# Experts 4 to 7 of a routed expert layer: all rows in one wide pass, behind both passes of experts 0 to 3

## Chip, cores and metric

The kernel runs on one core of one Trainium2 chip. The metric is the device time of one execution in microseconds; times are compared by the median of several runs.

## The reference, cut to what matters

The first half is a chunked state-space scan (Mamba-2 style) that gives 3072 tokens of 256 features. The second half routes each token to one of eight experts and is where the change is:

```python
def _moe_ref(x, w_gate, w1, w2):          # x: (3072, 256), w1: (8, 256, 1024), w2: (8, 1024, 256)
    logits = x @ w_gate
    expert_idx = np.argmax(logits, axis=1)
    logits_shift = logits - logits.max(-1, keepdims=True)
    probs = np.exp(logits_shift)
    probs /= probs.sum(-1, keepdims=True) + 1e-09
    gate_w = probs[np.arange(N), expert_idx]
    for e in range(E):
        mask = expert_idx == e
        h = np.maximum(x[mask] @ w1[e], 0.0)
        out[mask] = gate_w[mask, None] * (h @ w2[e])
```

With the inputs of this case the experts 0 to 7 get 372, 343, 418, 417, 336, 365, 415 and 406 tokens. All matmuls of the expert part are in float32.

## The kernel before, in words

**Scan and placing.** The scan runs over 12 steps of two chunks (the loop over `d`). As tokens are finished, their expert is chosen, their place among that expert's rows is counted (`rank`, `ranked`), and GpSimd writes each row by an indirect DMA (`place`, `to_places`) into `x_hbm`, a buffer in device memory with a region of NR rows for each expert. A row carries 256 features, the logits' parts and the token's number. Behind the last row of each expert, `empty_rest(e)` writes 128 empty rows, also by an indirect DMA from GpSimd; it must wait for the earlier reads of `x_hbm`, and a later read of `x_hbm` waits for it.

**Passes.** Every expert's rows are worked in two passes: the first takes 256 rows (P1), the second up to 192 more (P2). `jobs` lists them: jobs 0 to 7 are the first passes of experts 0 to 7, jobs 8 to 15 the second passes. A job goes through these steps:

- `m_load(i)` issues on SP's queue four DMAs for the rows (`xb`), one for their gate parts and token numbers (`lt`), and, for the first of a pair of second passes, two more (`lh`) for the rows behind the last full tile.
- `m_xT(i)` transposes `xb` to `xT` on VectorE in blocks of 32 by 32. For a second pass it transposes both jobs of the pair and then computes three gates (`gates`: VectorE, an exponential on ScalarE, VectorE again).
- The up stage: `up` makes two matmul calls for each of the 8 blocks of the hidden dimension, and ScalarE writes `hT` by a relu. In the trace each float32 matmul call is two instructions, so one expert's up stage is 32 instructions.
- The down stage `m_y(i)`: eight matmul calls for each tile of 128 rows, scaled by the gate (`put`) and sent to the output by an indirect DMA from GpSimd (`send`).

For second passes, `m_pair` handles two experts and has 17 programs for 128 to 192 rows in steps of 4. `over` computes the number of the program from the counts; TensorE and ScalarE load it (`number_of`) and branch. Rows above the full tile of 128 are done for both experts together in one half tile (`m_half`); there is none where the program's size is 128.

**Order.** The order of instructions on each engine is the order of the code; each engine works its own queue in that order. In the loop over `i` that does the first passes, a function `between(f)` is called behind the relu of block `f`. At `f == FT // 2` it issues, in this order: the weights of expert `i + 2` where they aren't there yet, the empty rows of two experts (`i` from 1 to 4), `m_load(i + 3)`, the load of a program number, and `m_xT(i + 1)`. So a first pass is loaded three experts ahead and transposed one ahead. Behind the first passes come four turns of `m_pair`, the loads and transposes of later pairs, and `m_y` of both jobs.

**Buffers.** `xb` and `xT` have four buffers, `lt` seven, `hT` three, `yo` (output tiles) three; PSUM has four banks for the up stage and two for the down stage. The weights of experts 0 to 2 have tiles of their own; those of experts 3 to 7 lie in memory that the scan has given up.

Of the kernel before, what the change touches and what calls it, by code (L numbers as in the profile page):

```python
# [38 lines left out]
SIZES = list(range(128, P2 + 1, 4))  # L39
SLACK, FEW = 64, 64  # L40
NR = N + 512
EW = 3
# [5 lines left out]
def ssd_then_moe(ctx, tc, xs_in, ae_in, wgx, w_gate, w1, w2, gx, gb, gc, ga, out):  # L48
# [41 lines left out]
    size_no = route.tile([1, E // 2], I32, name="size_no")  # L90
    steps = route.tile([1, len(SIZES) - 1], FP32, name="steps")
    spare = route.tile([1, 1], FP32, name="spare")
# [68 lines left out]
    def empty_consts():  # L161
        nc.gpsimd.memset(zrows, 0.0)
        none = sm.tile([128, 1], I32, name="none")
        nc.gpsimd.iota(none, pattern=[[0, 1]], base=N, channel_multiplier=0)
        nc.gpsimd.tensor_copy(zrows[:, TOK:TOK + 1].bitcast(I32), none)
        at_i = sm.tile([128, E], I32, name="at_i")
        nc.gpsimd.iota(at_i, pattern=[[NR, E]], base=0, channel_multiplier=1)
        nc.gpsimd.tensor_copy(at_r, at_i)
        steps_i = sm.tile([1, len(SIZES) - 1], I32, name="steps_i")
        nc.gpsimd.iota(steps_i, pattern=[[SIZES[1] - SIZES[0], len(SIZES) - 1]], base=P1 + SIZES[0],  # L170
                       channel_multiplier=0)
        nc.gpsimd.tensor_copy(steps, steps_i)
# [274 lines left out]
    def over():  # L447
# [9 lines left out]
        over_ = sm2.tile(sh, FP32, name="over")  # L457
        nc.vector.tensor_tensor(out=over_, in0=bc(most[:, :, None], sh), in1=bc(steps[:, None, :], sh), op=ALU.is_gt)
        nc.vector.tensor_reduce(most, over_, axis=AX, op=ALU.add)
# [15 lines left out]

    jobs = [(0, e) for e in range(E)] + [(1, e) for e in range(E)]
    ex = [dict() for _ in jobs]

    def m_load(i, engs=(nc.sync,)):

        p, e = jobs[i]
        r0, n = e * NR + P1 * p, (P1, P2)[p]
        xb = mo.tile([128, P1 // 32 * 64], FP32, name="xb", bufs=4)
        for c in range(4):
            engs[c % len(engs)].dma_start(out=xb[32 * c:32 * c + 32, 0:2 * n].rearrange("p (r z) -> p r z", z=64),
                              in_=x_hbm[r0:r0 + n, 64 * c:64 * c + 64].rearrange("(r j) z -> j r z", j=32))
        ex[i]["xb"] = xb[:, 0:2 * n].rearrange("p (r i k) -> p k r i", k=KT, i=32)
        lt = mo.tile([128, 2, MID], FP32, name="lt", bufs=7)[:, 0:2 - p]
        nc.sync.dma_start(out=lt, in_=x_hbm[r0:r0 + 128 * (2 - p), DM:W].rearrange("(t p) w -> p t w", p=128))
        ex[i]["lt"] = lt  # L490
        if p and e % 2 == 0:
            lh = mo.tile([128, 1, MID], FP32, name="lh", bufs=3)
            for u in range(2):
                q = r0 + u * NR + 128
                nc.sync.dma_start(out=lh[64 * u:64 * u + 64, 0], in_=x_hbm[q:q + 64, DM:W])
            ex[i]["lh"] = ex[i + 1]["lh"] = lh

    def gates(mid, n):

        sh = [128, n, E]  # L500
        l = mo.tile([128, 2, E], FP32, name="t_l", bufs=2)[:, 0:n]
        logits(l, mid)
        mx = mo.tile([128, 2], FP32, name="t_mx", bufs=2)[:, 0:n]
        nc.vector.tensor_reduce(mx, l, axis=AX, op=ALU.max)
        sub = mo.tile([128, 2, E], FP32, name="t_sub", bufs=2)[:, 0:n]
        nc.vector.tensor_tensor(out=sub, in0=l, in1=bc(mx[:, :, None], sh), op=ALU.subtract)
        nc.scalar.activation(sub, sub, func=ACT.Exp)  # L507
        se = mo.tile([128, 2], FP32, name="t_se", bufs=2)[:, 0:n]
        nc.vector.tensor_reduce(se, sub, axis=AX, op=ALU.add)  # L509
        nc.vector.tensor_scalar(out=se, in0=se, scalar1=1e-9, scalar2=None, op0=ALU.add)  # L510
        gt = mo.tile([128, 2], FP32, name="t_gt", bufs=8)[:, 0:n]
        nc.vector.reciprocal(gt, se)
        return gt

    def m_xT(i):
        p, e = jobs[i]
        n = (P1, P2)[p]
        for j in range(i, i + 1 + p):
            ex[j]["xT"] = mo.tile([128, KT, P1], FP32, name="xT", bufs=4)
            nc.vector.transpose(ex[j]["xT"][:, :, 0:n].rearrange("p k (r j) -> p k r j", j=32), ex[j]["xb"])  # L520
        if p:
            for j in range(i, i + 2):
                ex[j]["g"] = gates(ex[j]["lt"], 1)
            ex[i]["gh"] = gates(ex[i]["lh"], 1)

    H, Y, turn_no = [], [], [0, 0]
    hT_all = [mo.tile([128, FT, P1], FP32, name=f"hT{k}") for k in range(3)]

# [25 lines left out]
    def m_h(i, pp, between):  # L554
        p, e = jobs[i]
        n = (P1, P2)[p]
        ex[i]["hT"] = hT_next()
        for f in range(FT):
            q = up(ex[i]["xT"], w_sb[e][0], f, n, pp)
            nc.scalar.activation(ex[i]["hT"][:, f, 0:n], q, func=ACT.Relu)  # L560
            between(f)
# [19 lines left out]
    def m_y(i, pp, then=None):  # L581
        e = jobs[i][1]
        for t in range(2 - jobs[i][0]):
            p = y_next()
            for f in range(FT):
                nc.tensor.matmul(p, lhsT=ex[i]["hT"][:, f, 128 * t:128 * t + 128],  # L586
                                 rhs=w_sb[e][1][:, f * DM:f * DM + DM], start=(f == 0), stop=(f == FT - 1))
            put(p, ex[i]["lt"][:, t], ex[i]["g"][:, t:t + 1], i >= E - 1)
            if then:
                then()  # L590

    def m_half(i, n, yo):
        e = jobs[i][1]
        if n == 0:
            nc.scalar.mul(yo, zrows[:, 0:DM], 0.0)
            return
        p = y_next()
        for f in range(FT):
            for u in range(2):
                nc.tensor.matmul(p[64 * u:64 * u + n, :], lhsT=ex[i + u]["hT"][:, f, 128:128 + n],  # L600
                                 rhs=w_sb[e + u][1][:, f * DM:f * DM + DM], start=(f == 0), stop=(f == FT - 1))
        nc.scalar.mul(yo, p, ex[i]["gh"][:, 0:1])  # L602

# [11 lines left out]
    def m_pair(i, pp):  # L615

        e = jobs[i][1]
        for u in range(2):
            ex[i + u]["hT"] = hT_next()
        yo = mo.tile([128, DM], FP32, name="yh", bufs=2)  # L620
        at = list(turn_no)
        for c in tc.Switch(chosen(e // 2), len(SIZES), hint=f"pair{e // 2}"):
            turn_no[:] = at
            n = SIZES[c]
            for u in range(2):
                for f in range(FT):
                    q = up(ex[i + u]["xT"], w_sb[e + u][0], f, n, pp)
                    nc.scalar.activation(ex[i + u]["hT"][:, f, 0:n], q, func=ACT.Relu)  # L628
            m_half(i, max(0, n - 128), yo)
        turn_no[:] = [at[0] + 2 * FT, at[1] + 1]  # L630
        put_out(yo, ex[i]["lh"][:, 0])
# [82 lines left out]
    with tc.manual_schedule():  # L714
# [145 lines left out]
        idle(6, H[0])  # L860
        for e in range(EW, E):
            w_sb.append([w2pool.tile([128, KT * F], FP32, name=f"w{u + 1}_{e}") for u in range(2)])
        left = list(range(R0[LAST], NU))

# [3 lines left out]

        for i in range(E):
            def between(f):  # L870
# [19 lines left out]
                if f != FT // 2:  # L890
                    return
                if EW <= i + 2 < E:
                    for k in range(8):
                        load_w(i + 2, *divmod(k, 4))
                if i == 1:
                    over()
                if 1 <= i <= 4:
                    for e in range(2 * i - 2, 2 * i):
                        empty_rest(e)
                m_load(i + 3)  # L900
                if i == E - 1:
                    m_load(i + 4)
                if 2 <= i < 2 + E // 2:
                    number_of(i - 2)
                if i == E - 2:
                    more.append(nc.values_load(nk[0:1, 0:1], min_val=0, max_val=1,
# [3 lines left out]
            if i == 0:  # L910
                m_xT(1)
            if i < E - 1:
                m_y(i, pp, (lambda: more_places(2)) if i == 0 else None)
        tc.switch_hint(chosen(0), len(SIZES), "pair0")
        m_y(E - 1, pp)
        for k in range(E // 2):
            i = E + 2 * k
            m_pair(i, pp)
            if k + 1 < E // 2:
                tc.switch_hint(chosen(k + 1), len(SIZES), f"pair{k + 1}")  # L920
                for u in range(4, 6):
                    if i + u < len(jobs):
                        m_load(i + u)
                m_xT(i + 2)
            m_y(i, pp)
            m_y(i + 1, pp)
    with tc.If(more[0] > 0):
        with tc.tile_pool(name="gp", bufs=1) as gp:
# [64 lines left out]
```

## Time and profile before

| | us |
|---|---|
| median of 3 runs | 248.17 (247.75 to 251.34) |
| the profiled execution's own time | 247.47 |
| its span in the profile | 245.8 |
| TensorE matmul busy | 237.3 (97% of the span) |
| ScalarE, VectorE, GpSimd busy | 92.7, 88.5, 82.8 |
| up matmuls (L551) / down matmuls (L586) busy | 90.0 / 85.1 |
| DMA traffic | 39.75 MB, mean 162 GB/s |

The profile is of one execution. Busy time of an engine counts its computing instructions, not those that only wait or issue DMAs. "L551 PE MATMUL h_ps<-xT,w" is the instruction group of line 551 on TensorE, with what it writes and reads; an idle time in brackets is followed by what ended it. SP computes nothing: its lines are DMA issues, and the time of one is not the time of the transfer. PE is TensorE, ACT ScalarE, DVE VectorE, POOL GpSimd.

### The profile page before, as it was taken

How to read it: one execution, taken by the hardware profiler on the slowest of the kernel's cores; microseconds unless marked ns; L12 is line 12 of the kernel's file. 1: busy time of each engine (PE TensorE's matmuls, PEld its weight loads, DVE VectorE, ACT ScalarE, POOL GpSimd, SP SyncE). 2: the span in 40 equal slices, each digit the busy share in tenths (PEclk: the TensorE clock that was granted, in tenths of full speed). 3: DMA queues.
4: the chain of work that ended last, by engine and by line, in shares of the span. 5: the costliest groups of instructions: out<-in, count | busy, mean ns of one | idle time of the engine just before them, and what ended most of it. 6: DMA issues, size and time to landing. Idle time of an engine off the chain costs nothing. (4 is left out here: it accounts for less than half of the span.)

```text
span 245.8 us, 5525 instructions
## 1 busy us (share of the span) xinstructions
PE 237.3 (97%) x2021; PEld 201.3 (82%) x2021; DVE 88.5 (36%) x279; ACT 92.7 (38%) x312; POOL 82.8 (34%) x144
## 2 busy tenths in 40 slices
PE   8889899999999999999999999999999999999992
PEld 5567778777888888888888888888999969989781
DVE  4699879998520222020201102052316007040000
ACT  4656768981322224141422324131432502614200
POOL 2484688880038506060413330111113012013031
PEclk9999999999999999999999999999999999999999
DMA  6999979965932278696867779454303100001001
GB/s 174 327 328 323 332 250 302 291 263 102 274 141 97 112 144 274 189 256 217 235 243 213 272 168 311 87 99 82 73 13 68 32 15 29 27 4 40 3 16 45
DMA packets 36407, 39.75 MB, mean 162 GB/s; under 512 B 21947, under 2 KB 23806, under 8 KB 36352
## 3 DMA queue, kind: packets, MB, share of 16 engines
q1 hardware_dynamic: 32816, 30.24, 43.2%
q0 software_dynamic: 2880, 8.66, 9.3%
q8 instruction: 27, 0.44, 0.7%
q10 hardware_dynamic: 656, 0.18, 0.3%
q14 instruction: 28, 0.23, 0.3%
HBM read 29.72 MB, written 9.86 MB: 161 GB/s over the span
## 5 line engine op out<-in xcount | busy, mean ns | idle before, releaser
L551 PE MATMUL h_ps<-xT,w 128*128 128x256 f32 (+3 forms) x512 | 90.0, 334 | 0.3 <-ACT hT L628 0.3
L551 PEld LDWEIGHTS h_ps<-xT,w 128*128 128x128 f32 x512 | 80.8, 190 | 7.6 <-ACT hT L628 0.7
L586 PE MATMUL y_ps<-w,hT 128*128 128x256 f32 x384 | 85.1, 380 | 0.0
L586 PEld LDWEIGHTS y_ps<-w,hT 128*128 128x128 f32 x384 | 72.6, 190 | 10.5 <-issue 0.8
L564 POOL DMA_INDIRECT out_dram<-yo,lt x24 | 23.8, 991 | 58.1 <-DVE yo L571 31.3
L509 DVE TENSOR_REDUCE t_se<-t_sub 128x1 f32<-128x8 f32 (+1 forms) x20 | 3.3, 165 | 102.8 <-ACT t_sub L507 102.8
L560 ACT ACTIVATE hT<-h_ps 128x256 f32<-128x256 f32 x64 | 24.4, 384 | 29.4 <-PE h_ps L551 28.9
L282 DVE TENSOR_TENSOR M<-g,mask 128x1024 f32<-128x1024 f32 x24 | 28.2, 1218 | 3.8 <-PE g L277 3.6
L628 ACT ACTIVATE hT<-h_ps 128x128 f32<-128x128 f32 (+2 forms) x64 | 18.0, 292 | 24.1 <-PE h_ps L551 24.1
L421 POOL DMA_INDIRECT x_hbm<-rows,pos x24 | 23.9, 994 | 9.3 <-DVE pos L408 5.3
L573 ACT ACTIVATE yo<-y_ps,t_gt 128x256 f32<-128x256 f32 x14 | 6.6, 474 | 43.2 <-PE y_ps L586 43.2
L421 POOL DMA_INDIRECT x_hbm<-zrows,rest x8 | 7.7, 962 | 35.4 <-DMA lt<-x_hbm 24.9
L335 PE MATMUL y<-M,xp 128*32 128x128 f32 x384 | 15.3, 277 | 1.6 <-DVE M L282 1.3
L347 PEld LDWEIGHTS r<-turn,yT 128*128 128x128 f32 x88 | 12.2, 189 | 4.4 <-ACT yT L340 3.0
L261 ACT ACTIVATE cm<-xs_n,par 128x128 f32<-128x128 f32 x46 | 15.1, 419 | 1.5 <-DMA xs_n<-in_xs_dram 1.5
L347 PE MATMUL r<-turn,yT 128*128 128x160 f32 x88 | 14.9, 312 | 0.7 <-ACT ew L252 0.7
L564 POOL DMA_INDIRECT out_dram<-yh,lh x4 | 3.9, 983 | 33.1 <-ACT yh L602 21.2
L277 PE MATMUL g<-cm,xs_n 32*128 32x256 f32 x192 | 15.0, 423 | 0.0
L271 POOL TENSOR_TENSOR xp<-xs_n,Ei 128x256 f32<-128x256 f32 x20 | 12.1, 617 | 6.8 <-DVE last L241 3.6
L571 DVE TENSOR_SCALAR yo<-y_ps,t_gt 128x256 f32<-128x256 f32 x10 | 4.7, 483 | 24.2 <-PE y_ps L586 24.2
L340 ACT COPY yT<-y 128x512 f32<-128x512 f32 x12 | 7.0, 586 | 16.1 <-PE y L335 14.2
L520 DVE STREAM_TRANSPOSE xT<-xb 128x512 f32<-128x512 f32 (+1 forms) x16 | 9.8, 632 | 8.6 <-DMA xb<-x_hbm 7.1
(123 smaller groups left out, 156.2 us busy)
## 6 DMA issues: line engine op xcount, KB each, us to landing
w<-in_w_dram SPq DMA_DIRECT2D x64, 256.0 KB, 5.8
xs_n<-in_xs_dram SPq DMA_DIRECT2D x20, 320.0 KB, 5.8
xb<-x_hbm SPq DMA_DIRECT2D x30, 64.0 KB, 2.3
xb<-x_hbm SPq DMA_DIRECT2D x32, 48.0 KB, 2.4
xs_n<-in_xs_dram SPq DMA_DIRECT2D x4, 192.0 KB, 3.6
x_hbm<-zrows SPq DMA_DIRECT2D x1, 672.0 KB
lt<-x_hbm SPq DMA_DIRECT2D x8, 80.0 KB, 2.7
xs_n<-in_xs_dram SPq DMA_DIRECT2D x4, 128.0 KB, 2.3
```

The source lines that it names most:

```text
L261: nc.scalar.mul(t[:, u], st[n]["CT"], par[:, u:u + 1])
L271: eng.tensor_tensor(out=t, in0=st[n]["x"].rearrange("p (h d) -> p h d", d=D), in1=bc(Ei[:, n, :, None], [128, NH, D]), op=ALU.mult)
L277: nc.tensor.matmul(g_ps[:, q, n % 2], lhsT=st[n]["BT"][r], rhs=st[n]["cm"][r].rearrange("p u i -> p (u i)"), start=True, stop=True)
L282: nc.vector.tensor_tensor(out=t, in0=g_ps[:, :, n % 2].rearrange("p q (u i) -> p q u i", u=2), in1=bc(mask[:, None, None, :], [128, 4, 2, ...
L335: nc.tensor.matmul(y_ps[o:o + D, h // 4, CH * s:CH * s + CH], lhsT=st[n]["xp"][:, D * h:D * h + D], rhs=st[n]["M"][:, h], start=first, sto ...
L347: nc.tensor.matmul((to[s] if to else r_ps[:, s])[:, 256 * t:256 * t + 160], lhsT=sd[d]["yT"][:, t, CH * s:CH * s + CH], rhs=turn[:, t].rea ...
L421: s_ = nc.gpsimd.indirect_dma_start(out=x_hbm[:, :], out_offset=bass.IndirectOffsetOnAxis(ap=at, axis=0), in_=row, in_offset=None)
L551: nc.tensor.matmul(p[:, 0:n], lhsT=w[:, c:c + 128], rhs=xT[:, t, 0:n], start=(t == 0), stop=(t == KT - 1))
L560: nc.scalar.activation(ex[i]["hT"][:, f, 0:n], q, func=ACT.Relu)
L564: return nc.gpsimd.indirect_dma_start(out=out[:, :], out_offset=bass.IndirectOffsetOnAxis(ap=tok, axis=0), in_=yo[:, :], in_offset=None, b ...
L586: nc.tensor.matmul(p, lhsT=ex[i]["hT"][:, f, 128 * t:128 * t + 128], rhs=w_sb[e][1][:, f * DM:f * DM + DM], start=(f == 0), stop=(f == FT ...
L628: nc.scalar.activation(ex[i + u]["hT"][:, f, 0:n], q, func=ACT.Relu)
```

## The change

`jobs` becomes twelve: the first passes of experts 0 to 3 (0 to 3), the second passes of experts 0 to 3 (4 to 7), and one pass over all rows of each of the experts 4 to 7 (8 to 11). The wide passes are done in pairs by 17 programs for 320 to 448 rows in steps of 8, with three full tiles of 128 rows and a half tile above 384. They have row buffers of their own (`xw`, `xTw`, two each, 448 rows).

What moves with it:

- The loop of first passes ends at expert 3. In it `m_load(i + 3)` is, from `i = 1` on, a load of a second pass; `m_xT(4)`, for the pair of experts 0 and 1, is called in `between` of `i = 3`.
- Two program numbers are loaded at `i = 2` and two at `i = 3`.
- The empty rows of experts 6 and 7 are written in the first turn of pairs. In a turn `m_xT` is now called ahead of the loads.
- Experts 6 and 7 use the weight tiles of experts 0 and 1; their weights are loaded behind the down stage of the first pair.
- `hT` has two buffers of 448 columns for three of 256; `lt` has six for seven. Columns 320 to 383 of `hT` are set to zero once, by GpSimd, during the scan.
- `put` works on VectorE from the last first pass on, as before; that is now job 3.

The diff, cut to what the text speaks of:

```diff
+HE = E // 2
+PASS = ((0, P1, 2), (P1, P2, 1), (0, P1 + P2, 3))
+WSIZES = list(range(P1 + FEW, P1 + P2 + 1, 8))
...
-    steps = route.tile([1, len(SIZES) - 1], FP32, name="steps")
+    steps = route.tile([1, 2, len(SIZES) - 1], FP32, name="steps")
...
+        for hT in hT_all:
+            nc.gpsimd.memset(hT[:, :, WSIZES[0]:P1 + 128], 0.0)
+        steps_i = sm.tile([1, 2, len(SIZES) - 1], I32, name="steps_i")
+        for k, (z, b) in enumerate(((SIZES, P1), (WSIZES, 0))):
+            nc.gpsimd.iota(steps_i[:, k], pattern=[[z[1] - z[0], len(z) - 1]], base=b + z[0], channel_multiplier=0)
...
-        nc.vector.tensor_tensor(out=over_, in0=bc(most[:, :, None], sh), in1=bc(steps[:, None, :], sh), op=ALU.is_gt)
+        for k in range(2):
+            q = slice(E // 4 * k, E // 4 * k + E // 4)
+            nc.vector.tensor_tensor(out=over_[:, q], in0=bc(most[:, q, None], [1, E // 4, len(SIZES) - 1]),
+                                    in1=bc(steps[:, k:k + 1], [1, E // 4, len(SIZES) - 1]), op=ALU.is_gt)
...
-    jobs = [(0, e) for e in range(E)] + [(1, e) for e in range(E)]
+    jobs = [(p, e) for p in range(2) for e in range(HE)] + [(2, e) for e in range(HE, E)]
...
     def m_load(i, engs=(nc.sync,)):
         p, e = jobs[i]
-        r0, n = e * NR + P1 * p, (P1, P2)[p]
-        xb = mo.tile([128, P1 // 32 * 64], FP32, name="xb", bufs=4)
+        at, n, tiles = PASS[p]
+        r0 = e * NR + at
+        xb = mo.tile([128, (n if p == 2 else P1) // 32 * 64], FP32, name="xw" if p == 2 else "xb", bufs=2 if p == 2 else 4)
...
-        lt = mo.tile([128, 2, MID], FP32, name="lt", bufs=7)[:, 0:2 - p]
+        lt = mo.tile([128, 3, MID], FP32, name="lt", bufs=6)[:, 0:tiles]
...
     def m_xT(i):
         p, e = jobs[i]
-        n = (P1, P2)[p]
-        for j in range(i, i + 1 + p):
-            ex[j]["xT"] = mo.tile([128, KT, P1], FP32, name="xT", bufs=4)
+        n, tiles = PASS[p][1:]
+        for j in range(i, i + (2 if p else 1)):
+            ex[j]["xT"] = (mo.tile([128, KT, n], FP32, name="xTw", bufs=2) if p == 2 else
+                           mo.tile([128, KT, P1], FP32, name="xT", bufs=4))
             nc.vector.transpose(ex[j]["xT"][:, :, 0:n].rearrange("p k (r j) -> p k r j", j=32), ex[j]["xb"])
         if p:
             for j in range(i, i + 2):
-                ex[j]["g"] = gates(ex[j]["lt"], 1)
+                ex[j]["g"] = gates(ex[j]["lt"], tiles)
             ex[i]["gh"] = gates(ex[i]["lh"], 1)
...
-    hT_all = [mo.tile([128, FT, P1], FP32, name=f"hT{k}") for k in range(3)]
+    hT_all = [mo.tile([128, FT, P1 + P2], FP32, name=f"hT{k}") for k in range(2)]
...
-        for t in range(2 - jobs[i][0]):
+        for t in range(PASS[jobs[i][0]][2]):
...
-            put(p, ex[i]["lt"][:, t], ex[i]["g"][:, t:t + 1], i >= E - 1)
+            put(p, ex[i]["lt"][:, t], ex[i]["g"][:, t:t + 1], i >= HE - 1)
...
     def m_half(i, n, yo):
-        e = jobs[i][1]
+        p, e = jobs[i]
+        a = 128 * PASS[p][2]
+        n = max(0, n - a)
...
     def m_pair(i, pp):
...
-            n = SIZES[c]
+            n = (SIZES, WSIZES)[p - 1][c]
...
-        for e in range(EW, E):
+        for e in range(EW, E - 2):
             w_sb.append([w2pool.tile([128, KT * F], FP32, name=f"w{u + 1}_{e}") for u in range(2)])
+        w_sb.extend(w_sb[0:2])
...
-        for i in range(E):
+        for i in range(HE):
             def between(f):
...
                 if f != FT // 2:
                     return
-                if EW <= i + 2 < E:
+                if EW <= i + 2 < E - 2:
                     for k in range(8):
                         load_w(i + 2, *divmod(k, 4))
                 if i == 1:
                     over()
-                if 1 <= i <= 4:
+                if 1 <= i:
                     for e in range(2 * i - 2, 2 * i):
                         empty_rest(e)
                 m_load(i + 3)
-                if i == E - 1:
+                if i == HE - 1:
                     m_load(i + 4)
-                if 2 <= i < 2 + E // 2:
-                    number_of(i - 2)
-                if i == E - 2:
+                if i >= 2:
+                    for k in range(2):
+                        number_of(2 * i - 4 + k)
+                if i == HE - 1:
                     more.append(nc.values_load(nk[0:1, 0:1], min_val=0, max_val=1,
                                                skip_runtime_bounds_check_because="a truth value"))
                 m_xT(i + 1)
...
-        m_y(E - 1, pp)
+        m_y(HE - 1, pp)
         for k in range(E // 2):
-            i = E + 2 * k
+            i = HE + 2 * k
             m_pair(i, pp)
             if k + 1 < E // 2:
                 tc.switch_hint(chosen(k + 1), len(SIZES), f"pair{k + 1}")
+                m_xT(i + 2)
+                if k == 0:
+                    for e in range(E - 2, E):
+                        empty_rest(e)
                 for u in range(4, 6):
                     if i + u < len(jobs):
                         m_load(i + u)
-                m_xT(i + 2)
             m_y(i, pp)
             m_y(i + 1, pp)
+            if k == 0:
+                for e in range(E - 2, E):
+                    for j in range(8):
+                        load_w(e, *divmod(j, 4))
```

## The prediction

> **What bounds the kernel now.** I read the page first, then TensorE's timeline over the expert part, then the timelines of SP, GpSimd (POOL), VectorE and ScalarE over the same microseconds. The page:
>
> ```profile
> span 245.8 us, 5525 instructions
> PE 237.3 (97%) x2021; PEld 201.3 (82%) x2021; DVE 88.5 (36%) x279; ACT 92.7 (38%) x312; POOL 82.8 (34%) x144
> ```
>
> TensorE is busy 97% of the span, and no other engine 40%. Its timeline (start, length; a 256-wide stage of one expert is 32 matmul instructions):
>
> ```profile
> 103.88 7.07 PE L551 MATMUL h_ps<-xT,w 128*128 128x256 f32 x32
> 110.79 7.07 PE L586 MATMUL y_ps<-w,hT 128*128 128x256 f32 x32
> 117.70 7.07 PE L551 MATMUL h_ps<-xT,w 128*128 128x256 f32 x32
> ...
> 172.95 7.31 PE L551 MATMUL h_ps<-xT,w 128*128 128x128 f32 x64
> 180.09 7.07 PE L586 MATMUL y_ps<-w,hT 128*128 128x256 f32 x32
> 187.00 9.25 PE L551 MATMUL h_ps<-xT,w 128*128 128x164 f32 x64
> 196.19 3.65 PE L600 MATMUL y_ps<-w,hT 128*36 128x256 f32 x32
> ...
> 220.83 2.34 PE L551 MATMUL h_ps<-xT,w 128*128 128x160 f32 x16
> 223.44 6.79 PE L551 MATMUL h_ps<-xT,w 128*128 128x160 f32 x48 [0.27 <-ACT hT L628]
> ```
>
> From about 63 us on each stage begins where the last ended; the only gap is 0.27 us. So a saving in TensorE time counts in full, and every wait that reaches TensorE is a loss. Whether one does is decided by how early an expert's rows are there. SP (the loads) and POOL (the fills: indirect DMAs that write empty rows behind each expert's last one) give that:
>
> ```profile
> 100.86 1.81 SPq L485 DMA_DIRECT2D xb<-x_hbm  x4
> 102.71 0.45 SPq L489 DMA_DIRECT2D lt<-x_hbm  x1
> 103.21 3.81 SPq L204 DMA_DIRECT2D w<-in_w_dram  x8
> 114.01 1.81 SPq L485 DMA_DIRECT2D xb<-x_hbm  x4
> 115.86 0.45 SPq L489 DMA_DIRECT2D lt<-x_hbm  x1
> ```
>
> ```profile
> 105.77 0.96 POOL L421 DMA_INDIRECT x_hbm<-zrows,rest  x1 [7.46 <-DMA lt<-x_hbm]
> 107.04 0.96 POOL L421 DMA_INDIRECT x_hbm<-zrows,rest  x1 [0.23 <-issue]
> 119.14 0.96 POOL L421 DMA_INDIRECT x_hbm<-zrows,rest  x1 [8.48 <-DMA lt<-x_hbm]
> ```
>
> Counting calls of m_load in order, SP's 100.86 is job 4 and 114.01 is job 5. They form a ladder: the fills for experts 2 and 3 wait until job 4's load has landed (105.77), end on POOL at 108.00, and job 5's load is issued only once they are in HBM, 6.0 us later. Before, job 5 is the first pass of expert 5, whose matmuls start at 131.5: 17 us of slack. That slack is what the change spends.
>
> **The Trainium skill.** "TensorE: Matmul & The Clock Gate", Architectural detail: ScalarE and VectorE queues are strict FIFO. The trace agrees: the exponentials of the gates (L507) run between the two relus where the code puts them. "DMA: Bandwidth & Descriptors", Issuing engines are not separate DMA queues: DMAs of all issuers run on the same 16 DMA engines and interleave. The trace agrees: a fill issued with 2 MB of weights in flight takes 6.0 us to release SP, where the shortest of that line lands in 2.5. The clock-gate page, What's actually happening: an idle window of about 3.4 us halves TensorE's clock until about one busy window has passed. The trace shows no idle that long later on, but its start fits: the same 16 matmuls of L277 take 2.09 us at 4.62 and 1.15 at 9.84.
>
> **The change, part by part.**
>
> *Wider up matmuls (removed and added TensorE time).* From starts in the timeline: 256 columns cost 6.91/32 = 215.9 ns, 128 columns 7.14/64 = 111.6, 160 columns 9.33/64 = 145.8 (the gap in it). Removed for experts 4 to 7: four first passes, 27.6 us, and second passes of 7.14 and 9.33: 44.1 us. The sizes follow from the program's rule: pair (4,5) ran at 128 columns, its minimum; counting the reference's routing gives 336 and 365 rows, so 368 columns now and no half tile; pair (6,7) ran at 160, so 416, with the same half. No matmul that wide is in the trace. The line through 128 and 256 (0.815 ns a column) gives 307 and 346 ns; 0.833 plus 5 ns gives 312 and 352. 64 of each: 41.8 to 42.5 us. Gain 1.6 to 2.3; I take 2.0. The down stage keeps its count (three tiles an expert where it was two and one).
>
> *The early second pass of experts 0 and 1 (moved).* Job 5 is now the second pass of expert 1, and m_xT(4), which transposes jobs 4 and 5 and then computes three gates, stands in m_h(3) after relu 4 of 8, at about 107.5 us. That part of the code before is what stood at m_xT(8), with its data long landed:
>
> ```profile
> 162.20 1.04 DVE L520 STREAM_TRANSPOSE xT<-xb 128x384 f32<-128x384 f32 x2
> ```
> ```profile
> 166.73 0.21 ACT L507 ACTIVATE t_sub<-t_sub 128x8 f32<-128x8 f32 x1 [1.21 <-DVE t_sub L506]
> 166.85 0.91 ACT L560 ACTIVATE hT<-h_ps 128x256 f32<-128x256 f32 x3
> ```
>
> The order of instructions after the change has the three exponentials ahead of relus 5, 6 and 7 on ScalarE's queue. Even with data there those relus slipped to 166.85, 4.13 us after the second transpose began (162.72), and were just in time. Now the second transpose waits for job 5. Ladder: job 4 has two more DMAs (lh), which took 1.1 us at 160.03, so the fills start at 106.8 and not 105.8; job 5's load at 115.0; its four xb DMAs issued by 116.8, landed 2.4 us later (the median): 119.2. Relu 5 starts 119.2 + 4.1 = 123.3. TensorE finishes its up matmuls at 110.8, does f = 0 to 4 of m_y(3)'s first tile (10 x 0.216) until 112.95, and needs relu 5, ready at 123.7. Stall 10.7 us; nothing stands behind it that TensorE could run. Bounds: 8.5 (landing in 1.8, the shortest, and fills 1.6 us quicker) to 13 (landing 2.3 later, as next to weights).
>
> *Clock after the stall.* 10.7 us idle is far over the page's window. Estimate from the page: 3.4 to 5 us at half rate lose 1.7 to 2.5; I take 2.2; ends 0 (no drop) and 3.4.
>
> *Later steps.* Fills for 4 and 5 wait for job 5's lt (120.1), go out by 122.4, job 6 loads at 128.4 and job 7, with no fills between, at 132; landed about 136.5. m_y(3) ends about 130.7 and the pair of 0 and 1 (7.14, then 6.91) at 144.8, so xT(6) at 137.5 has 7 us in hand. Job 8 and 9 (fills of 6 and 7 at 138 to 140) land near 152, wanted at 164. The 4 MB for experts 6 and 7 overwrite w of 0 and 1 from 145 and are wanted 60 us later; the loads of jobs 10 and 11 queue behind them on SP, wanted 20 us later. All free. One small cost: before, the puts after the pair at 172.95 came 6.7 us after its up stage (exponentials again, 2.4 us of them issue on ScalarE); with three tiles in a row the third waits for the first's put: 0.3 to 0.5 us, I take 0.4.
>
> *Edits at nothing.* Two POOL memsets of 512 elements (zrows, 336, took 0.37: so 1.1 us) fall where POOL then idles 2.6 us; one iota and one compare likewise (VectorE waits 6.4 us after it). Two hT buffers for three: TensorE has read the older one before the relu's input exists. Second register loads on TensorE: one showed no gap.
>
> *Sum.* 10.7 + 2.2 + 0.4 - 2.0 = +11.3 us. The profiled execution's own 247.47 becomes 258.8; it lies 0.7 under the median 248.17, so 259.5 for the median.
>
> **Rivals.**
>
> *The cover holds* (0.12): job 5 lands by about 108.5 and only the gain is left, 248.17 - 2.0 + 0.4 = 246.6. It decides in the place of the ladder: if the fills did not wait for job 4, or landed in under 1 us. Three rungs of 5.2 to 6.0 us in the trace speak against it. Nothing gives 5 us of gain: the up stages hold 2.3 at most.
>
> *Half a stall* (0.10): the smaller loads drain sooner and relu 5 comes 5 us earlier, with no clock drop: 248.17 + 5.7 + 0.4 - 2.0 = 252.3. Against it: 2 MB of weights stand ahead of the fills as before.
>
> *A second stall* (0.13): job 7 comes over 7 us late behind weights of expert 5, or the wide pairs' rows do, for 5 us more: 264.5. For it: the ladder's next rung (127.39) exists; against: 7 us of slack.
>
> **How the numbers follow.** One stall at m_xT(4): 0.65, time 259.5, own range 254.4 (8.5, no clock loss, 2.3 gained, nothing else) to 263.4 (13, 3.4, 0.4, 1.6). The range 254 to 264.5 takes in most of the second stall. Over 2% (5.0 us, about what a measurement of this kernel can tell from no change): slower 0.65 + 0.13 + 0.04 of the half stall, 0.82; within 0.16; faster 0.02.
>
> **What would show it.** In the profile after: a TensorE gap of about 11 us at 113, ended by ScalarE's relu, VectorE's second 384-wide transpose waiting for the DMA of xb, matmuls at twice their time for some 4 us behind the gap; 64 up matmuls at about 307 ns and 64 at 350; no second gap over 1 us. No gap there, or one ended by weights, makes me wrong.

## The result, and the profile after

| | before | after |
|---|---|---|
| median, us | 247.96 (6 runs, 246.66 to 251.34) | 265.19 (6 runs, 260.16 to 267.68) |
| profiled execution, us | 247.47 | 265.47 |
| its span | 245.8 | 263.7 |

The ratio is 1.053, 95% interval 1.048 to 1.059: slower. All ratios here compare only the runs within 1.5% of a kernel's fastest, so they are not the quotients of the medians: that of after rests on 260.16 and 262.46, while the profile is of one of the longer runs, with which four later runs of the same kernel (e8 below) agree.

The lines of the page of after that answer to those of before, with the row of TensorE's granted clock and the queues that carry instructions:

```profile
span 263.7 us, 5178 instructions
PE 238.4 (90%) x1893; PEld 185.9 (71%) x1893; DVE 90.0 (34%) x260; ACT 82.9 (31%) x268; POOL 83.6 (32%) x147
...
PEclk9999999999999999995699999999999999999998
...
q8 instruction: 27, 0.44, 0.7%
...
q14 instruction: 29, 0.24, 0.3%
```

TensorE is busy about as long as before (238.4 for 237.3 us) in 128 fewer instructions; the span is 18 us longer. So the time went into standing still, and the clock row shows one dip, near 120 us. TensorE's timeline says where:

```profile
113.08 2.32 PE L596 MATMUL y_ps<-w,hT 128*128 128x256 f32 x10
125.15 7.01 PE L596 MATMUL y_ps<-w,hT 128*128 128x256 f32 x22 [9.74 <-DMA w<-in_w_dram]
132.00 7.31 PE L561 MATMUL h_ps<-xT,w 128*128 128x128 f32 x64
...
146.37 9.17 PE L561 MATMUL h_ps<-xT,w 128*128 128x164 f32 x64 [0.15 <-issue]
...
168.60 5.18 PE L561 MATMUL h_ps<-xTw,w 128*128 128x368 f32 x16 [2.38 <-DMA w<-in_w_dram]
175.33 15.11 PE L561 MATMUL h_ps<-xTw,w 128*128 128x368 f32 x48 [1.54 <-ACT hT L640]
190.27 7.07 PE L596 MATMUL y_ps<-w,hT 128*128 128x256 f32 x32
197.74 14.08 PE L596 MATMUL y_ps<-w,hT 128*128 128x256 f32 x64 [0.39 <-DVE yo L581]
211.65 22.51 PE L561 MATMUL h_ps<-xTw,w 128*128 128x416 f32 x64
```

There is the predicted gap behind ten matmuls of m_y(3), and a second stop at 168.6, where the pair of experts 4 and 5 begins. (The releaser "DMA w" at 125.15 had long landed; the weight loads' row names ScalarE's relu instead: "<-ACT hT L570 10.1".)

The ladder that led to the first gap, from the timelines of after, SP's first:

```profile
102.97 1.78 SPq L494 DMA_DIRECT2D xb<-x_hbm  x4
...
105.28 1.12 SPq L504 DMA_DIRECT2D lh<-x_hbm  x2
106.45 3.91 SPq L209 DMA_DIRECT2D w<-in_w_dram  x8
117.21 1.78 SPq L494 DMA_DIRECT2D xb<-x_hbm  x4
```

POOL's, the fills for experts 2 and 3:

```profile
108.81 0.96 POOL L426 DMA_INDIRECT x_hbm<-zrows,rest  x1 [8.42 <-DMA lh<-x_hbm]
110.08 0.96 POOL L426 DMA_INDIRECT x_hbm<-zrows,rest  x1 [0.22 <-issue]
```

VectorE's, the second transpose of the pair:

```profile
120.63 0.58 DVE L530 STREAM_TRANSPOSE xT<-xb 128x384 f32<-128x384 f32 x1 [10.20 <-DMA xb<-x_hbm]
```

ScalarE's, the first and last exponential and relus 5 to 7:

```profile
121.80 0.21 ACT L516 ACTIVATE t_sub<-t_sub 128x8 f32<-128x8 f32 x1 [10.73 <-DVE t_sub L515]
...
124.61 0.21 ACT L516 ACTIVATE t_sub<-t_sub 128x8 f32<-128x8 f32 x1 [1.20 <-DVE t_sub L515]
124.73 0.91 ACT L570 ACTIVATE hT<-h_ps 128x256 f32<-128x256 f32 x3
```

POOL's second fill ends at 111.04 and SP issues job 5's rows at 117.21, 6.2 us later; VectorE then transposes at 120.63, and the last three relus follow the last exponential, 4.10 us behind the transpose.

The whole difference of the profiled pair, from stage starts: the expert part begins 2.2 us later (62.75 for 60.56); the stretch 113.08 to 132.00 is 18.92 instead of 6.91 (+12.0: 9.9 standing, 2.1 at half clock); the second pair's exit and the wide entry +4.1 (2.54 and 1.54); the down stages of experts 4 to 7 +0.65, 0.39 of it a wait for the output tile; the two pairs of 0 to 3 and the ends +0.5; the wide up stages 1.5 less (1.8 in e3 and e6, where no stop falls into them). Together 17.95 of 18.0.

**The second stop.** The rows of the wide pair are not late: VectorE has transposed both jobs by 158.05, before the pair ahead is left. What is new there is 4 MB of weights, those of experts 6 and 7, that SP issues over the same microseconds. VectorE's timeline, then SP's:

```profile
156.65 1.40 DVE L530 STREAM_TRANSPOSE xTw<-xw 128x896 f32<-128x896 f32 x1 [3.92 <-DMA xw<-x_hbm]
```

```profile
154.58 11.75 SPq L209 DMA_DIRECT2D w<-in_w_dram  x16
```

ScalarE's timeline of after at the same place:

```profile
159.19 0.47 ACT L614 ACTIVATE yh<-y_ps,t_gt 128x256 f32<-128x256 f32 x1 [3.31 <-PE y_ps L612]
165.34 0.22 ACT L516 ACTIVATE t_sub<-t_sub 128x24 f32<-128x24 f32 x1 [5.67 <-issue]
...
174.80 1.58 ACT L640 ACTIVATE hT<-h_ps 128x368 f32<-128x368 f32 x4 [6.17 <-PE h_ps L561]
```

And of before, at the same point of the code:

```profile
202.74 0.21 ACT L507 ACTIVATE t_sub<-t_sub 128x8 f32<-128x8 f32 x1 [2.35 <-issue]
```

On leaving a pair's program ScalarE always pauses, with nothing that the profile shows to wait for: 2.35 us in before, 5.67 here. The Trainium skill has a page for it ("Runtime: NRT & Kernel Launch", Instruction fetch mechanics): a taken branch to a target outside the engine's instruction memory must fetch it by DMA before the engine goes on. The trace agrees. Its queue q14 carries "instruction" packets of 8 KB. At the exits of the pairs ScalarE runs again 1.9 to 2.3 us after one of them starts, in every trace of this case; what differs is when that packet starts: 0.1 to 0.6 us after ScalarE falls idle where little else moves, and 2.4 to 4.3 us after with megabytes of rows or weights in flight (1.2 in between, at e12's first exit). The DMA view of after from the start of the pause at 159.66, first 159.7 to 161.7 (packets, MB and share of the 16 engines):

```profile
q1 hardware_dynamic: 358, 0.66, 96.4%
```

The same, 162.2 to 162.8:

```profile
q1 hardware_dynamic: 113, 0.20, 101.4%
q14 instruction: 1, 0.01, 3.2%
```

And in e3, where those weights come later, at the same pause (157.4 to 158.4):

```profile
q1 hardware_dynamic: 55, 0.01, 9.8%
q14 instruction: 1, 0.01, 3.3%
```

In after no instruction packet moves in the first 2 us; the first of q14 comes at 162.4, the second at 163.2, and ScalarE runs again at 165.34, 2.2 us after the second. In e3 the one packet comes at 157.8, 0.4 us into the pause, which lasts 2.57. So in after the exponentials are late, and ScalarE's next program too (its packet at 172.5, 3.9 us after the last exponential, for the relus at 174.80 that end the 1.54). What TensorE itself waits for at 168.60 is taken up behind e12.

### The profile page after: what moved, and what is told of

Same layout as the page of the kernel before. It is cut to its first block, busy times and chain, and to the rows that moved or that the text cites. A ratio compares the mean times of both kernels' runs of the same rounds, so it can differ in the third digit from the quotient of the medians.

```text
span 263.7 us, 5178 instructions
## 1 busy us (share of the span) xinstructions
PE 238.4 (90%) x1893; PEld 185.9 (71%) x1893; DVE 90.0 (34%) x260; ACT 82.9 (31%) x268; POOL 83.6 (32%) x147
## 5 line engine op out<-in xcount | busy, mean ns | idle before, releaser
L596 PE MATMUL y_ps<-w,hT 128*128 128x256 f32 x384 | 87.0, 387 | 10.1 <-DMA w<-in_w_dram 9.7
L596 PEld LDWEIGHTS y_ps<-w,hT 128*128 128x128 f32 x384 | 73.9, 194 | 22.1 <-ACT hT L570 10.1
L561 PE MATMUL h_ps<-xTw,w 128*128 128x368 f32 (+1 forms) x128 | 42.8, 494 | 3.9 <-DMA w<-in_w_dram 2.4
L561 PE MATMUL h_ps<-xT,w 128*128 128x256 f32 (+2 forms) x256 | 45.3, 335 | 0.8 <-DVE xT L530 0.6
L561 PEld LDWEIGHTS h_ps<-xT,w 128*128 128x128 f32 x256 | 40.2, 190 | 4.8 <-DVE xT L530 1.1
L640 ACT ACTIVATE hT<-h_ps 128x128 f32<-128x128 f32 (+3 forms) x64 | 24.7, 395 | 60.1 <-PE h_ps L561 59.9
L561 PEld LDWEIGHTS h_ps<-xTw,w 128*128 128x128 f32 x128 | 24.2, 190 | 22.0 <-issue 12.6
L581 DVE TENSOR_SCALAR yo<-y_ps,t_gt 128x256 f32<-128x256 f32 x18 | 8.4, 482 | 62.6 <-PE y_ps L596 59.9
L570 ACT ACTIVATE hT<-h_ps 128x256 f32<-128x256 f32 x32 | 12.0, 382 | 15.8 <-PE h_ps L561 15.4
L518 DVE TENSOR_REDUCE t_se<-t_sub 128x1 f32<-128x8 f32 (+2 forms) x16 | 2.7, 167 | 36.7 <-ACT t_sub L516 36.7
L530 DVE STREAM_TRANSPOSE xTw<-xw 128x896 f32<-128x896 f32 x4 | 4.7, 1183 | 28.0 <-PE h_ps L561 19.4
```

The costliest lines, as they stand in the source:

```text
L561: nc.tensor.matmul(p[:, 0:n], lhsT=w[:, c:c + 128], rhs=xT[:, t, 0:n], start=(t == 0), stop=(t == KT - 1))
```

## The experiments

The theory: first, rows late by the ladder hold ScalarE's relus; second, weights of experts 6 and 7 in flight hold up the pair programs' entries and exits. Rivals: the order on ScalarE alone (e1); late rows or a new cost of the wide programs at the second stop (e3, e10); the memsets for the later start (e4). The chips differ (before: 248.12, 247.42, 255.38, 254.75), so only ratios and profiles are compared.

| | median us | before there | ratio, 95% | stops of TensorE from m_y(3) on, the main ones, us |
|---|---|---|---|---|
| e1 | 264.33 | 248.12 | 1.060 (1.052 to 1.067) | 4.96, 4.87, 1.80 |
| e2 | 257.19 | 248.12 | 1.038 (1.030 to 1.046) | 2.60, 1.81, 1.23, 0.96 |
| e3 | 260.88 | 248.12 | 1.054 (1.045 to 1.062) | 9.70, 0.89 |
| e4 | 266.58 | 248.12 | 1.074 (1.065 to 1.083) | 10.40, 2.72, 2.16 |
| e5 | 262.44 | 247.42 | 1.062 (1.054 to 1.070) | 6.74, 2.40, 2.06 |
| e6 | 250.93 | 247.42 | 1.016 (1.010 to 1.021) | 2.16, 0.42 |
| e7 | 264.42 | 247.42 | 1.069 (1.061 to 1.076) | 5.68, 2.72 |
| e8 | 265.41 | 247.42 | 1.075 (1.068 to 1.081) | 10.67, 3.38 |
| e9 | 257.86 | 255.38 | 1.008 (1.005 to 1.012) | 2.62, 0.39 |
| e10 | 257.47 | 255.38 | 1.010 (1.007 to 1.013) | 0.69, 0.32 |
| e11 | 270.23 | 255.38 | 1.058 (1.055 to 1.062) | 1.45, 1.40, 1.30 |
| e12 | 258.88 | 254.75 | 1.009 (1.006 to 1.012) | 3.13, 0.76 |

**e1: the pair's transposes and gates behind the up stage, not inside it.**

```diff
-                m_xT(i + 1)
+                if i < HE - 1:
+                    m_xT(i + 1)
...
+            if i == HE - 1:
+                m_xT(HE)
```

> The changed kernel with m_xT(4) called behind m_h(3) and not within it, so that its three exponentials stand behind relu 7 of job 3 on ScalarE. Queue theory (the stall at m_y(3) comes from the exponentials that stand ahead of relus 5 to 7 and wait for job 5's rows): m_y(3) runs through; ScalarE is then blocked until the third exponential at about 124.6, so TensorE stops for about 3 us after four up blocks of the first pair[...]; 9 us less than the changed kernel, about 252. Rival (TensorE lacks job 5's rows as such, wherever the transpose stands): the same gap of about 10 us moves to the first pair, and the time stays at 260 to 261.

m_y(3) runs through, but the time hardly changes; neither the 252 nor the single gap of about 10 us came. TensorE's timeline of e1:

```profile
125.07 8.46 PE L561 MATMUL h_ps<-xT,w 128*128 128x128 f32 x48 [4.96 <-ACT hT L640]
...
147.96 8.62 PE L561 MATMUL h_ps<-xT,w 128*128 128x164 f32 x48 [4.87 <-ACT hT L640]
```

The gap halves and moves to the first pair, and one of the same size comes at the second: VectorE can transpose job 7's rows, a rung further, only at 140.5. The order on ScalarE decides where the wait shows; the ladder sets how long.

**e2: the fills for experts 0 to 3 together at i = 1, and job 5 loaded there.**

```diff
-                if 1 <= i:
-                    for e in range(2 * i - 2, 2 * i):
-                        empty_rest(e)
-                m_load(i + 3)
+                for e in ((), range(0, 4), range(4, 6), ())[i]:
+                    empty_rest(e)
+                if i != 2:
+                    m_load(i + 3)
+                if i == 1:
+                    m_load(5)
```

> The changed kernel with the empty rows of experts 0 to 3 all written at i = 1 and job 5 loaded there too, ahead of expert 4's weights; those of 4 and 5 are written at i = 2. m_xT(4) stays where it is. Ladder theory (job 5's load is late because it waits for empty rows that wait for job 4's load): job 5 lands near 113 in place of 120, relu 5 starts near 117.5, the gap at m_y(3) shrinks from 9.7 to about 2.5 us and the clock stays up: 9 us less than the changed kernel, about 252. Rival (the load is late because the DMA engines are full of weights, whatever the order): job 5 lands within 2 us of 120 and the gap stays above 7 us.

TensorE's timeline of e2:

```profile
113.69 5.01 PE L596 MATMUL y_ps<-w,hT 128*128 128x256 f32 x22 [0.96 <-ACT hT L570]
...
158.56 21.72 PE L561 MATMUL h_ps<-xTw,w 128*128 128x368 f32 x64 [2.60 <-DVE t_gt L521]
```

The transpose of job 5 comes at 108.94 (120.63 in after), the first gap is 0.96, and the 22 matmuls behind it run at full clock. With the rung taken out, all but 0.96 us of the first stall is gone: its cause is shown. The edit also puts job 5's rows ahead of expert 4's weights; e5 separates the two. The second stop stays, and two of 1.23 and 1.81 us come ahead of it, so the time falls less than expected.

**e3: the weights of experts 6 and 7 behind the second pair.** A DMA of four bytes from that pair's last output tile holds them back.

```diff
-            if k == 0:
+            if k == 1:
+                tick = mo.tile([1, 1], FP32, name="tick")
+                nc.sync.dma_start(out=tick, in_=last_yo[-1][0:1, 0:1])
```

> The changed kernel with the weights of experts 6 and 7 loaded behind the last output tile of the second pair (a 4-byte DMA that reads this tile holds SP's queue until then), and not behind the first pair. Contention theory (the second stop, 2.4 us and 1.5 us at the entry of the first wide pair, and ScalarE's 5.7 us pause behind the second pair come from those 4 MB that are in flight just then): both stops vanish, ScalarE's pause falls to about 2.4 us, 4 us less than the changed kernel. Rival (the wide rows, their transposes or the gates are late): both stops stay, and the time changes by less than 1 us. The first stall, 9.7 us, is untouched in both.

TensorE's timeline of e3:

```profile
164.85 20.02 PE L562 MATMUL h_ps<-xTw,w 128*128 128x368 f32 x64 [0.89 <-DVE yo L582]
```

ScalarE's pause falls from 5.67 to 2.57 us and 3.0 us of the second stop are gone, with the wide pair's rows and the wide programs unchanged. The first stall is as in after (9.70). The ratio lies 2.1% under that of e8 (1.054 for 1.075), though level with after's own.

**e4: the two memsets later.** The calls move from the start of the kernel to a place behind the scan, in the first pass of expert 1.

```diff
-        for hT in hT_all:
-            nc.gpsimd.memset(hT[:, :, WSIZES[0]:P1 + 128], 0.0)
...
+                    for hT in hT_all:
+                        nc.gpsimd.memset(hT[:, :, WSIZES[0]:P1 + 128], 0.0)
                     m_load(2)
```

> The changed kernel with the two memsets of hT moved from the scan to the middle of job 1, where GpSimd is idle. If the memsets are why the expert part began 2.2 us later in the changed kernel's profile: first up matmul back at about 60.6 us and 2 us less. If that delay is from run to run or from elsewhere in the scan: the start moves by less than 0.7 us, and so does the time.

No gain. The expert part starts at 60.60 here, but between 60.1 and 61.1 in e1 to e3, which keep the memsets. In e8, the kernel after with no edit, it starts at 59.84. The 2.2 us at the start are a spread of runs whose cause stays open.

**e5: the weights of experts 4 and 5 behind job 7's rows.**

```diff
-                if EW <= i + 2 < E - 2:
+                if i == 1:
                     for k in range(8):
-                        load_w(i + 2, *divmod(k, 4))
+                        load_w(3, *divmod(k, 4))
...
+                    for k in range(16):
+                        load_w(4 + k // 8, *divmod(k % 8, 4))
```

> The changed kernel with one thing moved: the weights of experts 4 and 5 are loaded behind job 7's rows at i = 3, and not ahead of jobs 5 and 6. If the rungs of the ladder are long because the empty rows land among 2 MB of weights: a fill releases SP in 2.5 to 3.5 us in place of 6, job 5 lands near 113 to 115, the first gap falls from 9.7 to about 4 to 5 us, and job 7 lands by about 123, so that no gap comes at the second pair; 6 to 7 us less than the changed kernel. If the waits as such make the ladder (POOL's queue, SP's order), the gap stays above 8 us.

SP is released 1.65 us after POOL's fill (6.2 in after), so the weights are what delays a fill. The first gap falls to 6.74, not to the 4 to 5 expected: what is left is the rung itself, which e2 takes out. But 4 MB now fly while the pairs of 0 to 3 change over, and a new stop comes, ahead of matmuls at half clock (TensorE's timeline):

```profile
141.40 10.92 PE L561 MATMUL h_ps<-xT,w 128*128 128x164 f32 x64 [2.40 <-DVE t_se L518]
```

**e6: all of it together.** The fills for experts 0 to 5 at i = 1 with jobs 4 and 5 behind them, jobs 6 and 7 following by i, then the weights of 4 and 5 (edit of e5), and the edits of e1 and e3.

```diff
-                if 1 <= i:
-                    for e in range(2 * i - 2, 2 * i):
+                if i == 1:
+                    for e in range(6):
                         empty_rest(e)
-                m_load(i + 3)
+                    m_load(4)
+                    m_load(5)
```

> The changed kernel with the wide passes and all loads early: the empty rows of experts 0 to 5 are written together at i = 1, jobs 4 to 7 are loaded right behind them, the weights of 4 and 5 behind those, m_xT(4) stands behind m_h(3), and the weights of 6 and 7 come behind the second pair's last output tile. If stalls alone made the change slow: no gap over 1 us in the expert part, clock at full all along, 0.5 to 2 us under the kernel before (the up stages give 1.5, gates at the first wide pair take 0.4). If the wide matmuls or something else in the change is slow by itself: 3 us or more above it. If 4 MB of weights in flight at the first pair's entry and exit stop the engines there: gaps of 1 to 3 us between 118 and 133.

TensorE's timeline of e6:

```profile
132.52 10.84 PE L562 MATMUL h_ps<-xT,w 128*128 128x164 f32 x64 [2.16 <-DVE t_sub L515]
...
154.24 20.02 PE L562 MATMUL h_ps<-xTw,w 128*128 128x368 f32 x64 [0.19 <-issue]
```

From 1.075 (e8) to 1.016, with an interval of 1.010 to 1.021, which doesn't settle whether e6 is more than 2% slower. One stop of more than 0.5 us is left, where the weights of 4 and 5 fly, with 1.67 us of half clock behind it (10.84 for 9.17): 3.8 us, about what e6 lies above before (3.5). Without it the change would come out at no difference: an estimate that no run reached.

**e7 and e11: TensorE kept at work through the wait.** 75 and 120 matmuls without a use, before the eleventh of m_y(3)'s first tile; the rest is the kernel after.

```diff
+                if i == HE - 1 and t == 0 and f == 5:
+                    for _ in range(WARM):
+                        nc.tensor.matmul(r_ps[:, 0, 0:192], lhsT=ones_bf,
+                                         rhs=oh_all.rearrange("p n e -> p (n e)"), start=True, stop=True)
```

> The changed kernel with 75 small bf16 matmuls (128 by 192, results unused) placed in m_y(3) ahead of the sixth matmul of its first tile, where TensorE stands still for 9.7 us. If the clock drop behind the stall costs about 2 us: the 22 matmuls behind it take 4.8 us and not 6.8 to 7.7, and 2 us are saved. If the slow 22 matmuls have another cause (ScalarE's relus, weights in flight): they still take about 7 us.

> The changed kernel with 120 in place of 75 small bf16 matmuls in the first stall (75 took 6.35 us, so 120 take about 10.1 us), so that TensorE stands still for less than 2 us. If the clock drop follows from standing still: the 22 matmuls behind it take about 4.8 us in place of 6.9 to 7.6. If not: they take about 7 us again.

e7 says nothing: its 75 took 6.35 us and TensorE still stood 5.68, with the 22 matmuls at 6.94. In e11 the 120 cover the wait but for 1.30 (TensorE's timeline):

```profile
133.40 5.02 PE L601 MATMUL y_ps<-w,hT 128*128 128x256 f32 x22 [1.30 <-ACT hT L571]
```

5.02 for 7.01: about 2 us of the first stall are the clock's answer to standing still. The whole doesn't show those 2 us: e11's ratio, 1.058, lies between after's 1.053 and e8's 1.075.

**e8: the kernel after again**, on the chip of e5 to e7, with no edit.

> The changed kernel as it is, once more beside these, so that their times are compared on one chip: 260 to 266, with a first gap of 9.7 us and a second stop of 3 to 5 us at the first wide pair.

TensorE's timeline of e8:

```profile
168.42 21.72 PE L561 MATMUL h_ps<-xTw,w 128*128 128x368 f32 x64 [3.38 <-DVE t_gt L521]
```

Both stops are there again, the second as one piece of 3.38, and here it does cost clock (21.72 for 20.02). Two instruction packets start 2.9 and 3.9 us into ScalarE's pause of 5.93.

**e10: the kernel before with 4 MB of traffic at the change of pairs.** The weights of experts 0 and 1 are loaded once more behind the first pair.

```diff
             m_y(i + 1, pp)
+            if k == 0:
+                for e in range(2):
+                    for j in range(8):
+                        load_w(e, *divmod(j, 4))
```

> The kernel before, unchanged but for 4 MB more of DMA: the weights of experts 0 and 1 are loaded once more into their own tiles behind the down stage of the first pair of second passes, where the changed kernel loads those of 6 and 7; nothing reads them. If 4 MB in flight where a pair's program is left and the next entered stop the engines by themselves: ScalarE's pause behind the second pair grows from 2.4 to 5 or 6 us, TensorE stops 2 to 3 us at the third pair's entry and runs some 3 us at half clock, 3 to 5 us more than the kernel before. If the stop needs the wide programs or their rows: within 1 us of the kernel before.

TensorE's timeline of e10:

```profile
196.93 6.95 PE L551 MATMUL h_ps<-xT,w 128*128 128x164 f32 x48 [0.69 <-ACT hT L628]
```

Stops come without any wide program, but of 1.0 us in sum, and the kernel loses about 2 us (1.0%) of the 3 to 5 expected; the profile is of the shortest of its four runs. They come at the second pair's entry and not at the third's, and ScalarE's pauses at the exits stay at 2.5 us, their packets 0.4 us into them: SP issued the 4 MB from 180.99 to 195.48, between the exits at 187 and 208. It is at the entry between them that ScalarE's packet is late (2.2 us after the last exponential, 0.9 in before). So traffic is enough for a short stop where it meets a fetch; a stop of the size in after was not made in the kernel before.

**e9 and e12: the burst split and moved.** e9 is e6 with the weights of 5 behind the first pair and those of 6 and 7 behind the second; e12 also puts the rows of jobs 10 and 11 behind the second. The edit of e9 against e6, then what e12 adds:

```diff
-                    for k in range(16):
-                        load_w(4 + k // 8, *divmod(k % 8, 4))
+                    for k in range(8):
+                        load_w(4, *divmod(k, 4))
...
-            if k == 1:
+            if k < 2:
...
-                for e in range(E - 2, E):
+                for e in ((E - 3,), (E - 2, E - 1))[k]:
```
```diff
-                    if i + u < len(jobs):
+                    if k == 0:
...
+                if k == 1:
+                    m_load(10)
+                    m_load(11)
```

> The kernel of the run without waits, with its one remaining stop taken away: only expert 4's weights are loaded behind job 7's rows; expert 5's come behind the last output tile of the first pair, so that no more than 2 MB are in flight where the engines enter or leave a pair's program. If weights in flight make those stops: no gap over 0.6 us in the expert part, ScalarE's pauses behind the pairs near 2.4 us, 4 us less than the run without waits: 246.5 to 248, about 1 us under the kernel before. If the gap at the second pair's entry stays, its cause is another.

> The run with two triggers, with the rows of jobs 10 and 11 also loaded behind the second pair's last output tile (ahead of the weights of 6 and 7), so that neither rows nor weights should be in flight where the second pair is left and the first wide pair entered. If any DMA traffic there makes the stop: ScalarE's pause behind the second pair falls from 5.0 to about 2.5 us, the stop of 2.6 us and its half clock (1.7 us) vanish, the time lies 0.5 to 1.5 us under the kernel before. If the stop stays above 2 us, traffic isn't its cause in this kernel.

TensorE's timeline of e9:

```profile
161.27 21.72 PE L562 MATMUL h_ps<-xTw,w 128*128 128x368 f32 x64 [2.62 <-DMA xw<-x_hbm]
```

And of e12:

```profile
158.57 19.95 PE L562 MATMUL h_ps<-xTw,w 128*128 128x368 f32 x64
...
188.56 15.77 PE L598 MATMUL y_ps<-w,hT 128*128 128x256 f32 x64 [3.13 <-DVE yo L582]
```

In e9 the second pair begins without a stop and the wide pair has it; in e12 the wide pair begins clean, and the stop sits at its exit, where the 4 MB now fly (the instruction packet 2.8 us into a pause of 4.90). It follows the traffic from place to place. Neither did what was expected: e9 keeps a gap of 2.62 us (none over 0.6 expected), ScalarE's pause behind e12's second pair only falls from 4.96 to 4.37 (2.5 expected), and both stay about 1% slower than before. No version beat it.

**What TensorE waits for at the first wide pair.** The traces' other kind of instruction packets, 16 KB each on queue q8, tells. In after one of them starts only 0.4 us before the down stage ahead of the wide pair ends (the DMA view of after, 165.7 to 165.9):

```profile
q8 instruction: 1, 0.02, 28.3%
```

In e12 it starts 2.9 us before that end (155.7 to 155.9), and TensorE has no stop:

```profile
q8 instruction: 1, 0.02, 28.1%
```

In all twelve traces with a wide pair TensorE goes on 2.7 to 3.3 us after this packet starts. Measured from the end of ScalarE's last exponential it is anything from 1.3 us ahead (e12) to 1.6 us behind (e3). ScalarE's timeline of e12 has that exponential when TensorE has been at the wide pair for 1 us, since 158.57:

```profile
159.62 0.21 ACT L516 ACTIVATE t_sub<-t_sub 128x8 f32<-128x8 f32 x1 [1.24 <-DVE t_sub L515]
```

So the first part of the second stop (2.54 us in after) is a late fetch of TensorE's own, not ScalarE's exponentials, and the second part (1.54) is ScalarE's.

## Why the prediction was right, and where it was not

- **Direction and first stall: right.** 10.7 us predicted, 9.9 measured, with each step of the ladder in its place: fills at 106.8 predicted and 106.6 measured once the 2.2 us later start is taken off, job 5's load at 115.0 and 115.0, relus 4.1 us behind the second transpose and 4.10. e2 shows that the ladder makes it, e5 that the 2 MB of weights make the rung 6 us long.
- **Clock: right.** 2.2 predicted, 2.1 measured (6.85 us for 22 matmuls that take 4.75); e11 shows the cause.
- **Wider matmuls: right, a little small.** 310.3 (e3 and e6, which have no stop inside the stage) and 350.6 ns instead of 307 to 312 and 346 to 352: 1.8 us gained of the 2.0, and 1.5 in the profiled after, with its stop.
- **Puts at the first wide pair: right.** 0.4 predicted, a gap of 0.39.
- **"All free" for the later steps: wrong.** This is the step that failed. It asked when the weights of 6 and 7 and the rows are wanted, and they did come in time. It did not ask whom 4 MB in flight hold up: the instruction fetches of ScalarE and TensorE at the branches of the pair programs, 4.1 us in after. It also had them fly from 145; behind the rows of jobs 8 and 9 on SP's queue they were issued from 154.58 (152.4 with the later start taken off), over the very exit of the second pair (159.67). The rival with a second stall named late rows or weights of expert 5; its 264.5 lies near the median of 265.2, but by another mechanism, as e3 shows. "No second gap over 1 us" was wrong with it.
- **The sum.** +11.3 was predicted. The profiled pair shows +18.0: 4.1 is the second stop, 2.2 the start, and the rest small. By the ratio, after is at 261.2 (1.0532 x 247.96), inside the range; the median over all six runs is 0.7 above its upper end. That the ratio's figure lies inside is in part luck: the profiled pair is 18.0 us apart, and so are the medians of e8 and its before. In the profiled pair 6.3 of these (the second stop and the later start) have no term in the sum.
- **Memsets at nothing: right** (e4).

Left open: that q14 is ScalarE's queue and q8 TensorE's (inferred from their packets' times), why a fetch amid traffic starts as late as it does, and why the expert part starts at anything from 59.1 (e5) to 62.75 (after), and from 66.4 to 69.7 on the chips of e9 to e12.

## What to carry to other kernels

A reordering that saves little on the bound engine spends slack of the loads: for each wait that an in-order engine gets earlier, list what is queued behind it, and follow the rows back through every queue. When a large transfer is moved, ask not only when its data are wanted but what else is on the DMA engines meanwhile, and keep bursts of weights away from points where engines branch. Taking out one wait may only show the next one (e1); it took all the edits together (e6) to come near the kernel before (1.016), and what the change itself is worth is still an estimate.

## What the runs showed of the hardware

- A pair's exit costs ScalarE 2.1 to 2.6 us in quiet, and 4.4 to 6.4 with megabytes of rows or weights in flight (3.3 once, in between). It runs again 1.9 to 2.3 us after an instruction packet starts, early or late.
- An indirect write of empty rows released the next load after 6.2 us beside 2 MB of weights, and after 1.65 without.
- TensorE's clock halved after gaps shorter than the window of about 3.4 us that the Trainium skill gives ("TensorE: Matmul & The Clock Gate", What's actually happening): after 2.06 us in e5, for some 1.7 us of loss, though not after 2.38 in after. The page calls the window free-running, and the granted clock in the traces fits that. In the expert part it is at half for 3.41 us or two to four times that, and the spells of one run start whole multiples of 3.41 us apart. Counted in stretches of 3.41 us on that grid, the clock fell behind every one in which TensorE stood idle for 2.06 us or more, and behind none with 1.83 or less. The gap of e5 lies within one stretch; that of after is divided, 0.55 us in one and 1.83 in the next. (In the scan idle time alone doesn't decide: e11 and e12 have one such spell each behind a stretch with 0.7 to 0.8 us idle.) The stretches of e5, then of after (length, TensorE's busy time and instructions, granted clock, DMA share and GB/s):

```profile
162.51:165.92 3.41, 1.35 (x6) 1.00 1.04 256
165.92:169.34 3.42, 3.42 (x7) 0.50 1.12 159
```

```profile
163.36:166.77 3.41, 2.86 (x14) 1.00 1.04 370
166.77:170.18 3.41, 1.58 (x5) 1.00 1.07 286
170.18:173.60 3.42, 3.42 (x12) 1.00 1.22 189
```

- A float32 matmul instruction took 215.9 ns at 256 columns, 310.3 at 368 (e3, e6) and 350.6 at 416.
